# Mask matmuls, a new order of loads, and a regrouped first output phase in an attention and feed-forward kernel

## The chip, the cores and the metric

The kernel runs on one core of one Trainium2 chip. The metric is the device time of one execution in microseconds (us). Every execution also comes with the mean clock that was granted to TensorE, 1.0 being full speed. The five engines are TensorE (PE in the profile; PEld is its loading of weights), VectorE (DVE), ScalarE (ACT), GpSimd (POOL) and SyncE (SP). The program gives each of them a queue of instructions of its own. PSUM is the memory that the matmuls of this kernel write to; the kernel divides it into eight banks of 512 fp32 values in each of 128 partitions. SBUF is the memory that holds the other operands.

A ratio below is the mean time of one kernel's fast runs over the mean of the other kernel's fast runs of the same rounds, so it is not quite the ratio of the medians that stand beside it.

## The reference, cut to what matters

```python
# 8 batches, 8 heads, 512 local and 32 global positions, head size 64
k_all, v_all = concat(k_g, k_l), concat(v_g, v_l)
out_g = softmax(q_g @ k_all.T / 8) @ v_all            # global rows see everything
s_ll  = where(abs(i - j) <= 32, q_l @ k_l.T / 8, -1e9)  # local rows: a band of 65 ...
s_l   = concat(q_l @ k_g.T / 8, s_ll)                 # ... and the global columns
out_l = softmax(s_l) @ concat(v_g, v_l)
x = concat(out_g, out_l) as [8 * 544, 512]
h = x @ w_in                                          # 512 -> 2048, the "first layer" of a batch
out = (h * sigmoid(1.702 * h)) @ w_out                # 2048 -> 512, the "output phase" of a batch
```

## The kernel before

Four heads of a batch are a *quad*; quads 0 and 1 are batch 0, quads 2 and 3 batch 1. In the code `a` is the first quad of a batch and `c` the second. The steps of a quad, cut:

```python
psS = tile_pool("psS", bufs=1, PSUM)    # one tile of four banks: the score tile "s4"
psP = tile_pool("psP", bufs=4, PSUM)    # four single banks, taken in turn: pbank()

S(rnd)   # scores of half of the keys, 16 matmuls, into the score tile
X(rnd)   # exp of them, PSUM -> SBUF, on ScalarE (1.6 us)
M(rnd)   # times the band mask, on VectorE (0.9 us)
K, XK    # scores of the global keys, and their exp
ekU(u), U(u)  # attention times values: unit 0 is the denominator, 1 and 2 the values
R        # 1/denominator, spread: transpose, reciprocal, transpose, on VectorE (1.7 us)
XL(0), XL(1)  # xL = ov * rs, on VectorE; the input of the first layer
gg, eg, Gm, G # the same for the global rows: matmuls into og (Gm), division (G)
```

Some more names of the code: rq and rk are q and k as loaded, g the global rows, ov what U writes, sT and rs the first and last result of R, fc the number of a step of the first layer.

The global rows of batch 1 are loaded in fp32 by the SP queue and cast on ScalarE:

```python
def load_g32(b, names, hold=False, eng=None):
    ...
        t = g32[b, name] = consts.tile([128, 2, D], F32, ...)
        if hold:
            nc.vector.memset(t[:, :, 0:1], 0.0)   # the load waits for VectorE to get here
        (eng or nc.sync).dma_start(out=t, in_=s[:, 2 * b : 2 * b + 2, :])

def cast_g32(b, names):
    ...
            nc.scalar.activation(t[:, 2 * b : 2 * b + 2, :D], g32[b, name], AF.Copy)
```

The first layer and the output phase:

```python
def h_step(i, fc):                 # one of 16 steps of the first layer
    hp = pbank("hp")               # waits until the bank of four steps ago has been read
    h_mm(i, fc, hp, range(NKC))    # 4 matmuls of 512 columns
    ... ACT: th = tanh(hp);  DVE: gT[fc] = (th + 1) * hp

def o_mm(i, st):                   # one of 16 groups of 4 matmuls of 512 columns
    if first: ops[i, tci] = pbank("op")
    ...
```

The order of the start and of the first output phase, cut:

```python
c.S(0); c.X(0); a.M(1)
load_g32(1, "qkv", hold=True)            # at about 13 us
... c.S(1); c.X(1, halves=True) ... c.M(0) ... c.M(1, 0, 192); c.M(1, 192) ...
for fc in range(4, FC):                  # first layer of batch 0
    h_step(0, fc)
    if fc == 7:  cast_g32(1, "qkv")
    if fc == 10: transpose_g(2, 4)
...
osteps(0, (2, 2), (2, 3))                # first output phase, its second half
c.S(0); a.ekUs(c); c.XK(); c.X(0); a.U(0); a.R()
osteps(0, (3, 0))
a.U(1); a.U(2); c.S(1); a.Gm(); c.M(0); a.XL(0); a.XL(1); c.X(1); c.M(1); c.eg(); a.G()
osteps(0, (3, 1), (3, 2))
c.UG(); c.RXG()                          # the whole of the second quad's end
osteps(0, (3, 3))
```

The softmax here doesn't subtract the row's maximum and nothing guards it: scores larger than these inputs give would overflow.

## Time and profile before

The median was 313.07 us when the prediction was made (three runs, 312.66 to 313.36), and 312.94 with the run beside the changed kernel. The table gives the time at which each stage begins, read from the timeline as the start of its first matmul.

| stage | before, us |
|---|---|
| first scores | 7.90 |
| first layer, batch 0 | 20.19 |
| output phase, batch 0 | 34.41 |
| first layer, batch 1 | 57.08 |
| output phase, batch 1 | 73.19 |
| first layer, batch 2 | 93.10 |
| span of the profiled run | 310.7 |

The waits of TensorE (who waited, for whom, us in total, times, longest) are short:

```profile
PE w L162 <- DVE warm L158: 1.5, 1, 1.5
PE s L291 <- DVE kT L260: 0.9, 1, 0.9
PE kb L310 <- ACT e L319: 0.5, 1, 0.5
PE s L291 <- DVE q L263: 0.4, 1, 0.4
PE hp L457 <- DVE xL L421: 0.3, 1, 0.3
```

Four lines of the timeline of before (start, duration, engine, line, operation) show the way of the global rows of batch 1 and the seam between first layer and output phase. They are asked for at 12.95 us and cast at 28.19, without a wait; the output matmuls begin at 34.41, twenty of them in 4.48 us:

```profile
12.95 0.37 SPq L124 DMA_DIRECT2D g32q<-in_q_g_dram  x1
28.19 0.30 ACT L130 ACTIVATE rqg<-g32q 128x128 bf16<-128x128 f32 x1
28.59 0.30 ACT L130 ACTIVATE rvg<-g32v 128x128 bf16<-128x128 f32 x1
34.41 4.48 PE L482 MATMUL op<-w_out_sb,gT 128*128 128x512 bf16 x20
```

### The profile page before, as it was taken

What the parts mean: (1) busy time and instruction counts of PE and PEld (TensorE: products, weight loads), DVE (VectorE), ACT (ScalarE), POOL (GpSimd) and SP (SyncE); (2) the same over time, 40 slices, a digit from 0 to 9 for tenths busy, and PEclk for the clock granted to TensorE, in tenths of its full rate; (3) what the DMA queues carried; (4) which work ended last, traced back from release to release, by engine and by line L of the source; (5) the groups of instructions that cost most, each with busy time, mean ns of one, the idle gap of its engine ahead of it and who ended that gap; (6) DMA issues with size and microseconds to landing.
All of it is one profiled execution on the core that took longest, in us unless ns stands there. A gap on an engine that the chain in (4) does not pass through costs nothing.

```text
span 310.7 us, 7885 instructions
## 1 busy us (share of the span) xinstructions
PE 302.8 (97%) x3257; PEld 148.6 (48%) x3257; DVE 210.4 (68%) x463; ACT 167.3 (54%) x254; POOL 80.0 (26%) x131
## 2 busy tenths in 40 slices
PE   7899999999999999999999999999999999999995
PEld 6444444444554454444454455444454454446653
DVE  7887946869867866776957866776767855574320
ACT  4817465476536744565446735565556652563321
POOL 8822579677146000900045001200000000000000
PEclk9999999999999999999999999999999999999999
DMA  8999999999969212970279113901120012201123
GB/s 154 149 189 207 206 161 193 165 147 129 151 77 168 45 36 61 139 108 12 60 77 169 30 36 71 102 0 31 41 49 23 0 38 55 48 0 29 41 61 76
DMA packets 60099, 27.44 MB, mean 88 GB/s; under 512 B 43296, under 2 KB 51744, under 8 KB 60064
## 3 DMA queue, kind: packets, MB, share of 16 engines
q0 software_dynamic: 51536, 17.11, 50.7%
q1 hardware_dynamic: 7904, 9.12, 11.9%
q10 hardware_dynamic: 624, 0.72, 0.8%
q8 instruction: 25, 0.41, 0.5%
q14 instruction: 10, 0.08, 0.1%
HBM read 35.13 MB, written 8.91 MB: 142 GB/s over the span
## 4 chain that ended last, share of the span: by engine, by line
PE 91%; DVE 3%; ACT 2%; DMA 1%; POOL 1%; issue 0%; ACTq 0%; DVEq 0%; POOLq 0%
PE op L482 37%; PE hp L457 36%; PE s L291 6%; PE ov L389 5%; PE ov L367 3%; DMA rk<-in_k_l_dram 1%; PE s L457 1%; ACT e L322 1%; PE kb L310 1%; DVE e L329 1%; PE op L494 1%; PE s L310 1%; DVE gT L465 1%; PE s L406 1%; POOL rk L84 1%; PE ov L162 1%
## 5 line engine op out<-in xcount | busy, mean ns | idle before, releaser
L482 PE MATMUL op<-w_out_sb,gT 128*128 128x512 bf16 x528 | 121.9, 380 | 0.1
L465 DVE SCALAR_TENSOR_TENSOR gT<-th,hp 128x512 bf16<-128x512 f32 (+1 forms) x140 | 91.1, 655 | 43.0 <-ACT th L464 42.4
L457 PE MATMUL hp<-xL,w_in_sb 128*128 128x512 bf16 x496 | 108.6, 379 | 0.3 <-DVE xL L421 0.3
L464 ACT ACTIVATE th<-hp 128x512 f32<-128x512 f32 (+1 forms) x140 | 79.9, 573 | 43.7 <-PE hp L457 41.2
L457 PEld LDWEIGHTS <-w_in_sb 128*128 128x128 bf16 x576 | 56.1, 98 | 65.1 <-issue 1.2
L482 PEld LDWEIGHTS <-gT 128*128 128x128 bf16 x528 | 49.3, 98 | 56.2 <-issue 3.3
L322 ACT ACTIVATE e<-s 128x1712 bf16<-128x1712 f32 (+2 forms) x32 | 49.6, 1552 | 15.8 <-PE s L406 8.9
L496 ACT ACTIVATE ob<-op 128x512 f32<-128x512 f32 (+2 forms) x35 | 20.5, 585 | 61.6 <-PE op L482 59.1
L97 POOL DMA_DIRECT2D v<-in_v_l_dram x36 | 27.0, 757 | 96.2 <-PE s L406 88.9
L84 POOL DMA_DIRECT2D rk<-in_k_l_dram x64 | 34.9, 557 | 12.3 <-DMA w_in_sb<-in_moe_w_in_dram 4.7
L329 DVE TENSOR_TENSOR e<-e,mask 128x1408 bf16<-128x1408 bf16 (+2 forms) x33 | 28.0, 851 | 6.9 <-ACT e L322 6.7
L412 DVE STREAM_TRANSPOSE sT<-ov 128x512 f32<-128x512 f32 x16 | 11.4, 714 | 31.3 <-PE ov L389 31.3
L291 PE MATMUL s<-q,kT 32*128 32x200 bf16 (+1 forms) x512 | 21.3, 284 | 1.5 <-DVE kT L260 0.9
L421 DVE TENSOR_TENSOR xL<-ov,rs 128x512 bf16<-128x512 f32 x32 | 20.7, 685 | 2.2 <-PE ov L389 0.9
L291 PEld LDWEIGHTS <-kT 32*128 32x128 bf16 x512 | 10.9, 95 | 14.7 <-issue 9.1
L357 ACT ACTIVATE ek<-kb 128x512 bf16<-128x512 f32 x16 | 9.6, 600 | 8.4 <-PE kb L310 8.4
L389 PE MATMUL ov<-e,v 128*32 128x192 bf16 (+1 forms) x512 | 13.1, 240 | 0.0
L416 DVE STREAM_TRANSPOSE rs<-rT 128x512 f32<-128x512 f32 x16 | 11.4, 711 | 0.6
L260 DVE STREAM_TRANSPOSE kT<-rk 128x512 f32<-128x512 f32 (+1 forms) x17 | 11.4, 671 | 0.0
L263 DVE STREAM_TRANSPOSE q<-rq 128x512 f32<-128x512 f32 (+1 forms) x17 | 10.9, 647 | 0.0
L389 PEld LDWEIGHTS <-v 128*32 128x32 bf16 x512 | 9.8, 97 | 2.0 <-issue 2.0
L310 PE MATMUL kb<-q,kgT 32*32 32x512 bf16 x128 | 10.0, 385 | 0.5 <-ACT e L319 0.5
(71 smaller groups left out, 155.5 us busy)
## 6 DMA issues: line engine op xcount, KB each, us to landing
out_dram<-ob SPq DMA_DIRECT2D x132, 64.0 KB, 1.7
rk<-in_k_l_dram POOLq DMA_DIRECT2D x64, 64.0 KB, 4.0
v<-in_v_l_dram POOLq DMA_DIRECT2D x28, 128.0 KB, 4.5
rq<-in_q_l_dram POOLq DMA_DIRECT2D x6, 512.0 KB, 6.7
w_in_sb<-in_moe_w_in_dram POOLq DMA_DIRECT2D x4, 512.0 KB, 11.7
w_out_sb<-in_moe_w_out_dram POOLq DMA_DIRECT2D x4, 512.0 KB, 13.4
rq<-in_q_l_dram POOLq DMA_DIRECT2D x3, 256.0 KB, 7.9
q<-in_q_l_dram ACTq DMA_DIRECT2D x1, 512.0 KB, 3.9
```

The source lines that it names most:

```text
L84: nc.gpsimd.dma_start(out=loaded[b][0][32 * j : 32 * j + 32, u], in_=kf[b, j][:, u])
L97: nc.gpsimd.dma_start(out=vtiles[b % 2][p, s, :, :, :D], in_=vf[b, t][:, hs])
L291: nc.tensor.matmul(ps[j][:, off : off + n * nr], lhsT=self.k[p, 128 * c : 128 * c + 128, e], rhs=self.q[p, t0 : t0 + n, r0 : r0 + nr, e], ...
L322: nc.scalar.activation(e[:, :, lo:hi], self.ps[:, :, lo:hi], AF.Exp, scale=scale)
L329: nc.vector.tensor_mul(e, e, mask[:, rnd : rnd + 1, lo:hi].to_broadcast([128, 4, hi - lo]))
L389: nc.tensor.matmul(ov[32 * j : 32 * j + 32, :].rearrange("p (t r) -> p t r", t=16)[:, :, r0 : r0 + nr], lhsT=lv, rhs=self.E[c // 2][:, j, ...
L421: nc.vector.tensor_mul(self.x[:, 2 * self.u + h, :], self.st[1 + h], self.st["rs"])
L457: nc.tensor.matmul(hp[:, : width(i)], lhsT=w_in_c[:, fc // 8, kc, fc % 8 // 2, :, fc % 2], rhs=(xL[i] if i < B else xG)[:, kc, :], start=( ...
L464: nc.scalar.activation(th[:, :n], hp[:, :n], AF.Tanh, scale=0.851)
L465: nc.vector.scalar_tensor_tensor(gTs[i][:, fc, :n], in0=th[:, :n], scalar=1.0, in1=hp[:, :n], op0=ALU.add, op1=ALU.mult)
L482: nc.tensor.matmul(op, lhsT=gTs[i][:, fc, tci * 128 : tci * 128 + 128], rhs=w_out_sb[:, fc, :], start=(first and fc == 4 * f4), stop=(fc = ...
L496: nc.scalar.activation(ob[:, lo:hi], op[:, lo:hi], AF.Copy, scale=0.5)
```

## The change: its intent and the diff

The change means to take work out of the two places where TensorE was not full. It has three parts.

*Start.* The band masks of batch 0 are added to the scores on TensorE, as a large negative number, before exp, so that VectorE need not multiply. Half of the first keys come through SP in fp32, q in two pieces, v in eight, w_in in eight pieces, and the quarters of w_out come in a new order. The second scores of quad 1, with their mask matmuls, are cut in halves, as its exp already was.

*Global rows of batch 1.* They are loaded later, so that they do not get in the way of what the start needs; their casts and transposes move back with them.

*First output phase.* Scores of quad 3 come earlier, and its attention-times-values goes into the four banks of the score tile, so that the output matmuls can go on beside it. In the second layer quad 3's G is put after step 1, and some later pieces of work move back by one step (not in the cut below).

```diff
-    nc.scalar.dma_start(out=q32, in_=qf[0][:, 0])
+    for hf in range(2): ... nc.scalar.dma_start(out=q32[:, f], in_=qf[0][:, 0, f])
+    for j in range(4):
+        nc.sync.dma_start(out=k32[32 * j : 32 * j + 32], in_=kf[0, j][:, 0, 0:2])
 ...
-    keep(62, psP.tile([128, 512], F32, name="w", tag="p"), 128)
+    keep(40, psP.tile([128, 512], F32, name="w", tag="p"), 128)      # dummy matmuls
 ...
+        def B(self, rnd, split=False, cs=(0, 1)):      # masks: perm.T @ bias into the scores
+            ...
+                    nc.tensor.matmul(ps[j][:, w : w + 16 * WIN[c][1]], lhsT=perm, rhs=window(bias, c), ...)
 ...                                                    # start: the M of batch 0 go, B come
-    a.ekU(1, 3)
-    c.S(1)
-    c.X(1, halves=True)
+    c.B(1, cs=(0,)); c.S(1, added=True, cs=(0,)); c.X(1, part=0)
+    a.U(1); a.XL(0)
+    c.B(1, cs=(1,)); c.S(1, added=True, cs=(1,)); c.X(1, part=1)
 ...
-    load_g32(1, "qkv", hold=True)                      # was after c.X(0)
     for fc in range(4, FC):
         h_step(0, fc)
-        if fc == 7:
+        if fc == 5:
+            load_g32(1, "qkv", hold=True)
+            mps = pbank("mp") ...                      # mask of the later batches, once
+        if fc in (6, 7, 8, 9):
+            make_mask(fc - 6, mps)                     # on ScalarE
+        if fc == 11:
             cast_g32(1, "qkv")
-        if fc == 10:
+        if fc == 14:
             transpose_g(2, 4)
 ...                                                    # first output phase
+    c.S(0); c.X(0); c.M(0)
     osteps(0, (2, 2), (2, 3))
+    c.S(1); a.ekUs(c, 1); c.X(1); c.XK()
+    for unit in range(3): a.U(unit)
+    a.R(); c.M(1); c.eg()
+    pt = psS.tile([128, 4, 512], F32, name="s4")
+    a.Gm(pt[:, 0, 0 : D + 2])
+    osteps(0, (3, 0), (3, 1))
+    a.XL(0); a.XL(1)
+    c.ekUs(banks=[pt[:, unit + 1, :] for unit in range(3)])
+    for unit in range(3): c.U(unit)
+    c.R(); c.XL(0); c.XL(1)
+    a.G()
+    c.Gm(pt[:, 0, 256 : 256 + D + 2])
+    osteps(0, (3, 2), (3, 3))
```

More of the change, by code (lines that the diff above doesn't have):

```diff
@@ L135 @@
     q32 = ld.tile([128, 16 * D], F32, name="q32", bufs=1)
-    nc.scalar.dma_start(out=q32, in_=qf[0][:, 0])
-    load_g32(0, "qk")
-    load_g32(0, "v", eng=nc.scalar)
-    for j in range(4):
-        load_k(0, 0, j)
-    mk = consts.tile([32, 208], BF16)
-    nc.vector.memset(mk, 1.0)
-    for sg, base in ((1, 2 * W + 3), (-1, -3)):
-        nc.gpsimd.affine_select(
-            out=mk, in_=mk, pattern=[[-sg, 208]], compare_op=ALU.is_ge,
-            fill=0.0, base=base, channel_multiplier=4 * sg,
-        )
+    for hf in range(2):
+        f = slice(8 * D * hf, 8 * D * hf + 8 * D)
+        nc.scalar.dma_start(out=q32[:, f], in_=qf[0][:, 0, f])
+    k32 = ld.tile([128, 2, 4 * D], F32, name="k32", bufs=1)
+    load_g32(0, "q")
+    for j in range(4):
+        nc.sync.dma_start(out=k32[32 * j : 32 * j + 32], in_=kf[0, j][:, 0, 0:2])
+    load_g32(0, "kv")
+    step = consts.tile([128, 257], BF16)
+    nc.vector.memset(step, 1.0)
+    nc.gpsimd.affine_select(
+        out=step, in_=step, pattern=[[1, 257]], compare_op=ALU.is_ge,
+        fill=0.0, base=-65, channel_multiplier=-1,
+    )
+    for j in range(4):
+        nc.gpsimd.dma_start(out=loaded[0][0][32 * j : 32 * j + 32, 0, 2:4], in_=kf[0, j][:, 0, 2:4])
     load(0, (1,))
@@ L173, with rows4, window, make_mask @@
     WIN = ((0, 10), (6, 12), (14, 12), (22, 10))
-    mb = consts.tile([128, 16, 12], BF16)
     mask = consts.tile([128, 2, LW], BF16)
-    def make_mb():
-        for k in range(4):
-            nc.vector.tensor_copy(mb[32 * k : 32 * k + 32],
-                                  mk[:, 3 - k : 195 - k].rearrange("p (r t) -> p t r", t=16))
-    def make_mask():
-        at = 0
-        for c, (r0, nr) in enumerate(WIN):
-            lo = r0 - 8 * c + 2
-            nc.scalar.activation(
-                mask[:, c // 2, at : at + 16 * nr].rearrange("p (t r) -> p t r", t=16),
-                mb[:, :, lo : lo + nr], AF.Copy)
-            at = (at + 16 * nr) % LW
+    BIG = 262144.0
+    perm = consts.tile([128, 128], BF16)
+    band = consts.tile([128, 192], BF16)
+    bandt = consts.tile([128, 16, 12], BF16)
+    bias = consts.tile([128, 16, 12], BF16)
+    def rows4(t):
+        return t.rearrange("p (r t) -> p t r", t=4)
+    nc.vector.tensor_sub(perm.rearrange("p (t r) -> p t r", t=4), rows4(step[:, 65:193]), rows4(step[:, 64:192]))
+    nc.vector.tensor_sub(band, step[:, 65:257], step[:, 0:192])
+    nc.vector.tensor_scalar(bias, band.rearrange("p (r t) -> p t r", t=16), -1.0, BIG, op0=ALU.add, op1=ALU.mult)
+    def window(t, c):
+        lo = 0 if c else 2
+        return t[:, :, lo : lo + WIN[c][1]]
+    def make_mask(c, ps):
+        nr = WIN[c][1]
+        at = (0, 160, 0, 192)[c]
+        nc.scalar.activation(mask[:, c // 2, at : at + 16 * nr].rearrange("p (t r) -> p t r", t=16),
+                             window(ps[:, 0:192].rearrange("p (t r) -> p t r", t=16), c), AF.Copy)
     ones32 = consts.tile([128, 32], BF16)
@@ L214, in load_rest @@
     def load_rest():
-        load_v(0)
-        for part in range(2):
-            cs = slice(part * (d_ff // 2), (part + 1) * (d_ff // 2))
+        for u in range(2):
+            load_v(0, (u,))
+        for c4 in range(4):
             for u in range(2):
-                nc.gpsimd.dma_start(out=w_in_sb[:, part, 2 * u : 2 * u + 2, :], in_=w_in_r[u][:, :, cs])
-        for g4 in range(4):
+                lo = c4 % 2 * 512
+                nc.gpsimd.dma_start(out=w_in_sb[:, c4 // 2, 2 * u : 2 * u + 2, lo : lo + 512],
+                                    in_=w_in_r[u][:, :, 512 * c4 : 512 * c4 + 512])
+        for g4 in (1, 0, 2, 3):
             nc.gpsimd.dma_start(
@@ L223, in load_rest @@
                 in_=w_out_r[:, 2 * g4 : 2 * g4 + 2, :])
-            if g4 == 1:
+            if g4 == 0:
                 load(1, (0,))
@@ L249, in __init__ @@
             self.E = [None, None]
+            self.bk = {}
             self.st = {}
@@ L275, in ext, with S @@
                     qgT[:, self.Q, : n * nr].rearrange("p (t r) -> p t r", t=n))
-        def S(self, rnd, split=False, warm=0):
-            if split:
-                ps = [pbank("s") for _ in range(4)]
-                keep(warm, ps[0])
-            else:
-                pt = self.spt(rnd)
-                ps = [pt[:, j, :] for j in range(4)]
-            off = 0
-            for c in (2 * rnd, 2 * rnd + 1):
+        def B(self, rnd, split=False, cs=(0, 1)):
+            if cs[0] == 0:
+                self.bk[rnd] = [pbank("s") for _ in range(4)] if split else self.spt(rnd)
+            ps = self.bk[rnd] if split else [self.bk[rnd][:, j, :] for j in range(4)]
+            for c in [2 * rnd + i for i in cs]:
+                w = (40, 200, 36, 228)[c]
+                for j in range(4):
+                    nc.tensor.matmul(ps[j][:, w : w + 16 * WIN[c][1]], lhsT=perm, rhs=window(bias, c),
+                                     start=(c == 2 * rnd), stop=False, skip_group_check=True)
+        def S(self, rnd, split=False, added=False, cs=(0, 1)):
+            if not added and cs[0] == 0:
+                self.bk[rnd] = self.spt(rnd)
+            ps = self.bk[rnd] if split else [self.bk[rnd][:, j, :] for j in range(4)]
+            for c in [2 * rnd + i for i in cs]:
+                off = (0, 200, 0, 228)[c]
                 r0, nr = WIN[c]
@@ L294, in S @@
                             rhs=self.q[p, t0 : t0 + n, r0 : r0 + nr, e],
-                            start=(e == 0), stop=(e == 1), skip_group_check=True,
+                            start=(e == 0 and not added), stop=(e == 1), skip_group_check=True,
                         )
-                off += n * nr
+            if cs[0] == 0:
+                self.E[rnd] = att.tile([128, 4, RW + 32], BF16, name="e%d" % rnd)
             if split:
                 self.gk(ps[2][:, RW : RW + 32], self.qg)
-            self.ps = ps if split else pt
-            self.E[rnd] = att.tile([128, 4, RW + 32], BF16, name="e%d" % rnd)
+            self.ps = self.bk[rnd]
         def gk(self, out_, rhs, e=None):
@@ L312, in gk, with X @@
                                      start=(ee == 0), stop=(ee == 1), skip_group_check=True)
-        def X(self, rnd, halves=False):
+        def X(self, rnd, part=None):
             e = self.E[rnd]
@@ L320, in X @@
                 return
-            for lo, hi in ((0, 228), (228, RW)) if halves else ((0, RW),):
+            for lo, hi in ((0, RW),) if part is None else ((228 * part, 228 + 200 * part),):
                 nc.scalar.activation(e[:, :, lo:hi], self.ps[:, :, lo:hi], AF.Exp, scale=scale)
-            if rnd == self.gr:
+            if rnd == self.gr and not part:
                 nc.scalar.activation(e[:, 2, RW:], self.ps[:, 2, RW : RW + 32], AF.Exp, scale=scale)
@@ L349, in spt, with gg @@
             return self.pt
-        def gg(self):
-            self.gr = 0
-            self.gk(self.spt(0)[:, 2, RW : RW + 32], self.qg)
+        def gg(self, rnd=0):
+            self.gr = rnd
+            self.gk((self.ps if rnd else self.spt(0))[:, 2, RW : RW + 32], self.qg)
         def XK(self):
@@ L357, in XK, with ekU @@
             nc.scalar.activation(self.ek, self.kb, AF.Exp, scale=scale)
-        def ekU(self, unit, warm=0):
-            ov = self.st[unit] = pbank("ov")
+        def ekU(self, unit, warm=0, ov=None):
+            if ov is None:
+                ov = pbank("ov")
+            self.st[unit] = ov
             keep(warm, ov)
@@ L368, in ekU, with ekUs @@
                                  start=True, stop=False, skip_group_check=True)
-        def ekUs(self, nxt=None):
+        def ekUs(self, nxt=None, rnd=0, banks=(None, None, None)):
             if nxt:
-                nxt.gg()
+                nxt.gg(rnd)
                 nxt.K(0)
-            self.ekU(0)
+            self.ekU(0, ov=banks[0])
             if nxt:
                 nxt.K(1)
-            self.ekU(1)
-            self.ekU(2)
+            self.ekU(1, ov=banks[1])
+            self.ekU(2, ov=banks[2])
         def U(self, unit):
@@ L393, in U, with Gm @@
                     )
-        def Gm(self, nxt=None):
-            og = nxt.pt[:, 0, RW : RW + D + 2] if nxt else pbank("og")
+        def Gm(self, og=None):
+            if og is None:
+                og = pbank("og")
             for c in range(5):
@@ L439, in UG @@
                 self.U(unit)
-            self.Gm(nxt)
+            self.Gm(nxt and nxt.pt[:, 0, RW : RW + D + 2])
         def RXG(self):
@@ L517, in cast_q @@
         nc.scalar.activation(rq[:, 0, f], q32[:, f], AF.Copy)
-    make_mb()
     cast_q(0)
     cast_q(1)
-    make_mask()
+    nc.scalar.activation(rk[:, 0, 0:2], k32, AF.Copy)
     cast_g32(0, "q")
@@ L533 @@
     load_rest()
-    a.S(0)
+    a.B(0)
+    a.B(1, split=True)
+    a.S(0, added=True)
     a.X(0)
-    a.S(1, split=True, warm=4)
+    a.S(1, split=True, added=True)
     a.X(1)
     c.ext()
+    c.Tk()
     cast_g32(0, "v")
-    c.Tk()
+    c.Tq()
+    c.B(0)
     a.K()
     a.XK()
-    a.M(0)
-    c.Tq()
+    c.S(0, added=True)
     c.gg()
-    c.S(0)
     c.X(0)
-    a.M(1)
-    load_g32(1, "qkv", hold=True)
     a.eg()
-    c.K(0)
+    c.K()
+    c.XK()
     a.ekU(0)
-    c.K(1)
-    c.XK()
     a.U(0)
     a.R()
-    a.ekU(1, 3)
-    c.S(1)
-    c.X(1, halves=True)
-    a.ekU(2, 4)
-    a.U(1)
+    nc.vector.tensor_copy(bandt, band.rearrange("p (r t) -> p t r", t=16))
+    a.ekU(1, 2)
+    c.B(1, cs=(0,))
+    c.S(1, added=True, cs=(0,))
+    c.X(1, part=0)
+    a.U(1)
+    a.XL(0)
+    c.B(1, cs=(1,))
+    c.S(1, added=True, cs=(1,))
+    c.X(1, part=1)
+    a.ekU(2)
     a.U(2)
+    a.XL(1)
     a.Gm()
-    c.M(0)
-    a.XL(0)
-    c.M(1, 0, 192)
-    c.M(1, 192)
-    a.XL(1)
     gTs[0] = moe.tile([128, FC, TB], BF16, name="gT")
@@ L595 @@
         h_step(0, fc)
-        if fc == 7:
+        if fc == 5:
+            load_g32(1, "qkv", hold=True)
+            mps = pbank("mp")
+            nc.tensor.matmul(mps[:, 0:192], lhsT=perm, rhs=bandt.rearrange("p t r -> p (t r)"),
+                             start=True, stop=True)
+        if fc in (6, 7, 8, 9):
+            make_mask(fc - 6, mps)
+        if fc == 11:
             cast_g32(1, "qkv")
-        if fc == 10:
+        if fc == 14:
             transpose_g(2, 4)
@@ L615 @@
     osteps(0, (0, 1), (0, 0), (1, 1), (1, 0), (2, 1))
-    c.ext()
     a.S(0)
@@ L623 @@
     a.eg()
+    c.T()
+    c.ext()
     osteps(0, (2, 0), (0, 2), (0, 3))
@@ L626 @@
     a.X(1)
-    c.T()
     a.M(1)
     osteps(0, (1, 2), (1, 3))
+    c.S(0)
+    c.X(0)
+    c.M(0)
     osteps(0, (2, 2), (2, 3))
-    c.S(0)
-    a.ekUs(c)
+    c.S(1)
+    a.ekUs(c, 1)
+    c.X(1)
     c.XK()
-    c.X(0)
-    a.U(0)
+    for unit in range(3):
+        a.U(unit)
     a.R()
-    osteps(0, (3, 0))
-    a.U(1)
-    a.U(2)
-    c.S(1)
-    a.Gm()
-    c.M(0)
+    c.M(1)
+    c.eg()
+    pt = psS.tile([128, 4, 512], F32, name="s4")
+    a.Gm(pt[:, 0, 0 : D + 2])
+    osteps(0, (3, 0), (3, 1))
     a.XL(0)
     a.XL(1)
-    c.X(1)
-    c.M(1)
-    c.eg()
+    c.ekUs(banks=[pt[:, unit + 1, :] for unit in range(3)])
+    for unit in range(3):
+        c.U(unit)
+    c.R()
+    c.XL(0)
+    c.XL(1)
     a.G()
-    osteps(0, (3, 1), (3, 2))
-    c.UG()
-    c.RXG()
-    osteps(0, (3, 3))
+    c.Gm(pt[:, 0, 256 : 256 + D + 2])
+    osteps(0, (3, 2), (3, 3))
     a, c = nq[2]
@@ L658 @@
         h_step(1, fc)
+        if fc == 1:
+            nq[1][1].G()
         if fc == 2:
@@ L662 @@
             a.Tq()
-        if fc == 7:
+        if fc == 8:
             transpose_g(4, 6)
             a.ext()
-        if fc == 9:
+        if fc == 10:
             a.S(0)
@@ L671 @@
             a.X(0)
-        if fc == 12:
+        if fc == 13:
             a.M(0)
```

## The prediction

> **What bounds it now.** The page gives TensorE 302.8 of 310.7 us busy, and the chain of waits is TensorE for 91%. From 57 us on the chain is back-to-back matmuls: 64 of 512 columns take 13.81 us, 215.8 ns each[...]. No step there changes; only the first 57 us can give time.
>
> - Start: the timeline has the first scores at 7.90 us, after a DMA of rk (3.08 to 7.06 in the chain), and the first layer at 20.19. Between them useful TensorE work is about 7 us (four score rounds of 0.60, two K of 0.43, six ekU+U of 0.5, small ones): 5 us are waits and 11 dummy matmuls of 0.22. Mask multiplies of 0.89 us stand in the chain.
> - First output phase: 34.41 to 57.08, 22.7 us. The same work later (107.1 to 127.7) takes 20.6. So 2.1 us are lost here, around the unoverlapped second quad (e, sT, rs, xL, 51.3 to 57.1).
> - DMA: full in the page's slices to about 85 us, at 150 to 210 GB/s. By issue plus time to landing: v of batch 0 is in at 15.7, w_in in four parts at 18.8, 21.7, 24.6, 27.4 (the last just as fc 8 needs it), w_out at 30, 32.5, 37.7, 40.5, q of quad 3 at 42.9, where its transpose starts at once. Just in time throughout.
>
> **What the change does.** Removes four mask multiplies (0.85 to 0.95 us DVE each) and 1.33 us of mask copies; adds 16 matmuls per quad of 160 to 192 columns, 0.59 us per round (estimate: columns at 215.8 ns per 512). Quad 0's run while TensorE waits for data anyway; quad 1's largely while ACT runs exp (1.6 us). Mask building moves into the first layer (about 1.3 us ACT, which has 0.27 us slack per step).
>
> The first scores now wait for q and half of k: estimated 6.8 us (-1.1). [...] Then exp of 1.6, 1.8, 0.6, 1.8, 0.6, 1.65 us on ACT becomes the chain; I get the first layer at 17.5 (-2.7). w_in in eighths should arrive at 17.1, 18.6, 20, 21.4...: enough, with up to 0.5 us of wait at fc 4. The first layer ends near 31.6 instead of 34.4.
>
> The regrouped phase by itself would recover nearly all of its 2.1 us, but loads move only 0.5 to 1 us earlier: w_out's last quarter near 40 and q of quad 3 near 42.4 now stop TensorE, about 1 us each. I expect 21.5 to 22.7 us for the phase and the second layer at 53.7 (-3.4) at best, -2 if DMA holds it. Behind that everything shifts.
>
> **Prediction: 310.0 us**, 80% range 307.9 to 311.9. Faster by over 2% 0.04, within 2% 0.95, slower 0.01.
>
> **What would show it.** First scores at 6.4 to 7.2 us; first layer at 17 to 18; its waits small, on w_in if any; waits in the output phase on w_out or q/k transposes; later phases unchanged (20.6, 13.8 us); ACT's lag in the first layer about 1 us more without stopping TensorE.
>
> **What would make it wrong.** Loads come clearly earlier because late g loads and smaller pieces free the engines: then up to -5 us. Or w_in in eighths costs bandwidth or POOL issue time: the first layer starves and the gain falls to 1 us or less. Mask matmuls on the chain (1.2 us) would cost a third of the start's gain.

The two passages that are cut hold no term of the sum. It stands as it was on record: the first layer 2.7 us earlier, the second layer 3.4 at best and 2 if the loads hold it, all behind it shifted; from 313.07 us that is 309.7 to 311.1, and 310.0 was put on record.

## More of the kernel before

The page of the kernel before, its parts 1 and 2. In part 2 each digit is one of 40 slices of the span, in tenths:

```profile
span 310.7 us, 7885 instructions
PE 302.8 (97%) x3257; PEld 148.6 (48%) x3257; DVE 210.4 (68%) x463; ACT 167.3 (54%) x254; POOL 80.0 (26%) x131
...
PEclk9999999999999999999999999999999999999999
DMA  8999999999969212970279113901120012201123
```

TensorE is the bound, the DMA engines are full for the first quarter, and the clock stays at 9 tenths or more in every slice.

## The result, and the profile after

The changed kernel took 327.74 us (median of four runs, 325.68 to 329.89) against 312.94 (four runs); the ratio is 1.0472, with a 95% interval of 1.0399 to 1.0546. I had predicted a small gain; it is a loss of 15 us.

| stage begins, us | before | after | stage before it became longer by |
|---|---|---|---|
| first scores | 7.90 | 7.55 | |
| first layer, batch 0 | 20.19 | 21.69 | 1.5 (start) |
| output phase, batch 0 | 34.41 | 42.41 | 6.5 (first layer, 6.2 of it a wait at its end) |
| first layer, batch 1 | 57.08 | 71.70 | 6.6 (output phase) |
| output phase, batch 1 | 73.19 | 89.19 | 1.4 |
| first layer, batch 2 | 93.10 | 109.10 | 0.0 |
| span | 310.7 | 326.5 | -0.2 after that |

So everything was lost before 89 us, in the places that were to gain. The page after shows a clock that falls three times in the first 75 us:

```profile
span 326.5 us, 7905 instructions
PE 307.9 (94%) x3259; PEld 150.0 (46%) x3259; DVE 207.0 (63%) x458; ACT 168.2 (52%) x255; POOL 84.3 (26%) x138
...
PEclk9799969969999999999999999999999999999999
DMA  8999999999712951198028901580121011200213
```

Two waits of TensorE are new and long (the page's first group of output matmuls shows the same 6.2 us):

```profile
PE op L509 <- DVE gT L492: 6.2, 1, 6.2
PE s L433 <- DVE xg L455: 3.6, 1, 3.6
PE s L301 <- ACT e L346: 1.6, 2, 1.0
```

**The first wait.** The waits of ScalarE between 30 and 45 us, and the timeline around them, tell where it comes from:

```profile
ACT rkg L130 <- DMA g32k<-in_k_g_dram: 2.5, 1, 2.5
ACT rqg L130 <- DMA g32q<-in_q_g_dram: 2.5, 1, 2.5
ACT rvg L130 <- DMA g32v<-in_v_g_dram: 1.7, 1, 1.7
```

```profile
28.88 0.38 SPq L124 DMA_DIRECT2D g32q<-in_q_g_dram  x1
35.93 0.31 ACT L130 ACTIVATE rqg<-g32q 128x128 bf16<-128x128 f32 x1 [2.54 <-DMA g32q<-in_q_g_dram]
38.78 0.31 ACT L130 ACTIVATE rkg<-g32k 128x128 bf16<-128x128 f32 x1 [2.54 <-DMA g32k<-in_k_g_dram]
40.84 0.31 ACT L130 ACTIVATE rvg<-g32v 128x128 bf16<-128x128 f32 x1 [1.75 <-DMA g32v<-in_v_g_dram]
41.06 0.58 ACT L491 ACTIVATE th<-hp 128x512 f32<-128x512 f32 x1
42.41 6.47 PE L509 MATMUL op<-w_out_sb,gT 128*128 128x512 bf16 x20 [6.20 <-DVE gT L492]
```

The rows are now asked for at 28.88 to 31.25 us and land 7.0 to 9.6 us later. Their casts stand in ScalarE's queue after step 11 and wait for them. The tanh of step 12 stands behind the casts and runs at 41.06 instead of near 33.7, when step 11's was done. The tanh of steps 12 to 15, with the product on VectorE (gT) behind it, is what gives back the four PSUM banks that the steps hold, and the first output matmul needs one of them. So TensorE stands from 36.2 to 42.4. The order is the program's in this trace: the casts at 35.93, 38.78 and 40.84, and tanh at 41.06, directly behind the last of them.

**The second wait.** The timeline before the second layer shows the second Gm (L433, into the score tile) wait for VectorE:

```profile
64.40 0.72 DVE L439 STREAM_TRANSPOSE sT<-s 128x512 f32<-128x512 f32 x1 [1.04 <-PE s L415]
66.19 1.29 DVE L448 TENSOR_TENSOR xL<-s,rs 128x512 bf16<-128x512 f32 x2
67.58 0.28 DVE L455 TENSOR_SCALAR xg<-s,rg 128x64 bf16<-128x64 f32 x1
67.92 0.41 PE L433 MATMUL s<-v,e 128*32 128x66 bf16 x16 [3.57 <-DVE xg L455]
68.32 3.59 PE L509 MATMUL op<-w_out_sb,gT 128*128 128x512 bf16 x8
```

**The clock.** After both waits the matmuls are slow: 20 output matmuls take 6.47 us (4.48 before), 8 take 3.59 (the eight at 53.31 us in the same phase took 1.90). The view by stretches (busy us of each engine with its number of instructions, then the granted clock, the DMA share and GB/s) shows the clock at one half:

```profile
35.00:40.00 5.00, 1.21 (x6) 0.46 (x5) 0.00 (x0) 0.62 (x2) 2.29 (x5) 0.97 1.15 205
40.00:45.00 5.00, 2.59 (x7) 0.92 (x7) 3.10 (x5) 3.19 (x6) 3.07 (x5) 0.50 1.44 166
65.00:70.00 5.00, 2.08 (x25) 0.88 (x25) 2.97 (x8) 0.00 (x0) 2.61 (x4) 0.70 0.88 126
66.60:67.00 0.40, 0.00 (x0) 0.00 (x0) 0.40 (x2) 0.00 (x0) 0.00 (x0) 0.95 0.71 90
67.00:67.40 0.40, 0.00 (x0) 0.00 (x0) 0.40 (x2) 0.00 (x0) 0.00 (x0) 0.50 1.04 78
```

At the first wait the granted clock was 1.00 from 39.0 to 39.4 us, 0.81 from 39.4 to 39.8 and 0.50 from 39.8 to 46.4; TensorE had been without a matmul since 36.2. At the second it fell sooner, after 2.6 us without a matmul (the last two lines above; see the last section). The prediction has no term for the clock.

**Theories.** Theory 1: the two waits and the half clock after each make nearly all of the loss, and each wait has one cause that can be taken away by itself (the place of the casts in a queue; a tile that two writers share). Its rivals: the loads as a whole are late, so that w_out, q or k would hold TensorE in any case; TensorE needs the late rows themselves; the wait before Gm is only the wait for xL that would come a little later; the low clock has another cause than idleness.

### The profile page after: what moved, and what is told of

The parts are those of the page before. It is cut to its first block, busy times and chain, and to the rows that moved or that the text cites. A ratio compares the mean times of both kernels' runs of the same rounds, so it can differ in the third digit from the quotient of the medians.

```text
span 326.5 us, 7905 instructions
## 1 busy us (share of the span) xinstructions
PE 307.9 (94%) x3259; PEld 150.0 (46%) x3259; DVE 207.0 (63%) x458; ACT 168.2 (52%) x255; POOL 84.3 (26%) x138
## 4 chain that ended last, share of the span: by engine, by line
PE 84%; DMA 6%; DVE 3%; POOL 3%; ACT 2%; issue 1%; ACTq 0%; SPq 0%; DVEq 0%
PE op L509 36%; PE hp L484 30%; PE s L315 6%; PE ov L415 5%; DMA g32v<-in_v_g_dram 3%; PE ov L393 3%; DMA rq<-in_q_l_dram 2%; DVE gT L492 1%; DMA rk<-in_k_l_dram 1%; PE s L484 1%; POOL rk L84 1%; POOL v L97 1%; PE kb L334 1%; ACT e L346 1%; ACT th L491 1%; PE s L433 1%
## 5 line engine op out<-in xcount | busy, mean ns | idle before, releaser
L509 PE MATMUL op<-w_out_sb,gT 128*128 128x512 bf16 x528 | 125.6, 388 | 6.3 <-DVE gT L492 6.2
L484 PE MATMUL hp<-xL,w_in_sb 128*128 128x512 bf16 x496 | 109.8, 381 | 0.0
L509 PEld LDWEIGHTS <-gT 128*128 128x128 bf16 x528 | 50.1, 99 | 65.3 <-issue 14.1
L97 POOL DMA_DIRECT2D v<-in_v_l_dram x40 | 28.9, 731 | 112.6 <-PE s L433 105.0
L84 POOL DMA_DIRECT2D rk<-in_k_l_dram x60 | 32.5, 548 | 8.9 <-DMA w_in_sb<-in_moe_w_in_dram 4.4
L353 DVE TENSOR_TENSOR e<-e,mask 128x1408 bf16<-128x1408 bf16 x28 | 24.4, 872 | 8.3 <-ACT e L346 8.3
L448 DVE TENSOR_TENSOR xL<-ov,rs 128x512 bf16<-128x512 f32 x30 | 19.4, 686 | 3.7 <-PE ov L415 2.1
L415 PE MATMUL ov<-e,v 128*32 128x160 bf16 (+1 forms) x480 | 12.3, 239 | 0.0
```

The lines of the kernel that those rows point to most:

```text
L84: nc.gpsimd.dma_start(out=loaded[b][0][32 * j : 32 * j + 32, u], in_=kf[b, j][:, u])
L97: nc.gpsimd.dma_start(out=vtiles[b % 2][p, s, :, :, :D], in_=vf[b, t][:, hs])
L353: nc.vector.tensor_mul(e, e, mask[:, rnd : rnd + 1, lo:hi].to_broadcast([128, 4, hi - lo]))
L415: nc.tensor.matmul(ov[32 * j : 32 * j + 32, :].rearrange("p (t r) -> p t r", t=16)[:, :, r0 : r0 + nr], lhsT=lv, rhs=self.E[c // 2][:, j, ...
L448: nc.vector.tensor_mul(self.x[:, 2 * self.u + h, :], self.st[1 + h], self.st["rs"])
L484: nc.tensor.matmul(hp[:, : width(i)], lhsT=w_in_c[:, fc // 8, kc, fc % 8 // 2, :, fc % 2], rhs=(xL[i] if i < B else xG)[:, kc, :], start=( ...
```

## The experiments

There were seventeen kernels, all correct (a planned e3 was not run). Times are medians; "before" in each job was 312.7 to 313.3 us.

**e1: the early load put back.** From the changed kernel:

```diff
     c.X(0)
+    load_g32(1, "qkv", hold=True)
     a.eg()
 ...
         if fc == 5:
-            load_g32(1, "qkv", hold=True)
```

> The changed kernel, with one thing undone: the global rows of batch 1 are loaded after exp of quad 1 (as before the change), not from step 5 of the first layer. Theory 1 (ScalarE stands in its queue at the casts of those rows, 35.3 to 40.8 us, so tanh of steps 12 to 15 comes late, the PSUM banks stay taken and TensorE stands 6.2 us): that wait goes, and with it the half clock after it; 319.0 to 320.5 us. Rival (the loads as a whole are late; w_out or q and k would hold TensorE anyway): the wait only moves to another load, 325 us or more.

Measured: 319.65 us (ratio 1.021). The wait before the output phase is gone, and the first 20 output matmuls are at full clock again (the trace has a record of 19 of them):

```profile
35.94 4.48 PE L509 MATMUL op<-w_out_sb,gT 128*128 128x512 bf16 x19
```

8.1 us of the 14.8 are explained. No wait for w_out, q or k came in its place, so the first rival falls.

**e2: G ahead of R.** From the changed kernel:

```diff
         c.U(unit)
+    a.G()
     c.R()
     c.XL(0)
     c.XL(1)
-    a.G()
     c.Gm(pt[:, 0, 256 : 256 + D + 2])
```

> The changed kernel, with the division of quad 2's global rows (G) put on VectorE ahead of quad 3's R and XL, so that the second Gm, which writes the same PSUM bank, need not wait for the end of VectorE's queue. Theory 1: TensorE's wait of 3.6 us before the second Gm goes, and most of the half clock after it (about 2 us); 322 to 323.5 us. Rival (TensorE would wait for xL of quad 3 a little later anyway, since R and XL end at 67.5 us): at most 1.5 us, 326 us.

Measured: 329.30 us, no gain; my expectation was wrong. The wait did not go away, it changed its partner. The timeline of e2 has the second Gm here:

```profile
69.25 0.41 PE L433 MATMUL s<-v,e 128*32 128x66 bf16 x16 [3.83 <-DVE xL L448]
```

XL reads banks 2 and 3 of the score tile. Gm writes to bank 0. That does not look like a wait for a bank.

**e4: dummies in the first gap.**

```diff
+    keep(28, pts[0][:, 0, :])      # 28 matmuls of 512 columns into bank 0 of the score tile
     osteps(0, (0, 1), (0, 0), (1, 1), (1, 0), (2, 1))
```

> The changed kernel with 28 dummy matmuls of 512 columns (6 us at full clock) put on TensorE between the first layer and the first output phase, where it stands idle 6.2 us. If the half clock after the gap is a cost of its own, made by the idleness: the first 20 output matmuls take 4.3 us instead of 6.5, and the time falls by 2 to 3 us to 325. If the lower clock has another cause, or costs nothing that the chain sees: no change, 327.7, or longer if the dummies don't fit.

Measured: 335.15 us. The test of the clock failed, because the dummies did not run in the gap but after it:

```profile
42.99 8.20 PE L166 MATMUL s<-warm 128*128 128x512 bf16 x27 [7.67 <-DVE gT L535]
```

They were written to bank 0, whose last reader was long done; they waited for L535, which at that point reads banks 2 and 3 of the same tile. Together with e2 this gives the second theory its form: a write to a tile waits for every read of the tile that was issued before it, whichever banks it touches. If that is so, it is an order that the program's dependency tracking makes, not one that the data need; e16 tests it directly.

**e5: the late load alone, in the kernel before.**

```diff
-    load_g32(1, "qkv", hold=True)
 ...
-        if fc == 7:
+        if fc == 5:
+            load_g32(1, "qkv", hold=True)
+        if fc == 11:
             cast_g32(1, "qkv")
-        if fc == 10:
+        if fc == 14:
             transpose_g(2, 4)
```

> The kernel before, with this one part of the change: the global rows of batch 1 are loaded from step 5 of the first layer, cast after step 11 and transposed after step 14. Theory 1 (lateness of this load is enough by itself): TensorE stands 5 to 7 us before the output phase, and 319 to 323 us result. Rival (it takes the smaller pieces and the mask work on ScalarE as well): under 315 us.

Measured: 320.85 us (ratio 1.025), with TensorE's wait of 6.5 us before the output phase. This move of a load of 192 KB, with its casts and transposes, costs 8 us by itself, the half clock included:

```profile
41.10 7.34 PE L482 MATMUL op<-w_out_sb,gT 128*128 128x512 bf16 x19 [6.51 <-DVE gT L465]
```

The mask work on ScalarE and the smaller pieces are not needed for it.

**e6: e1 with Gm issued early.**

```diff
         c.U(unit)
+    c.Gm(pt[:, 0, 256 : 256 + D + 2])
     c.R()
 ...
     a.G()
-    c.Gm(pt[:, 0, 256 : 256 + D + 2])
```

> e1 (early global rows) with quad 3's Gm issued before its R and XL, not after. Theory 1 (a write to one bank of the four-bank score tile waits for every read of that tile that was issued before it, whichever bank it reads: in e2 the wait went over from G to XL, in e4 the dummies in bank 0 waited for a read of banks 2 and 3): now nothing has read the tile's ov banks before Gm, so the 3.6 us go and most of the half clock after it, less up to 0.9 us of wait for xL at the second layer: 314 to 315.5 us against e1's 319.65. Rival (TensorE waits for xL there in any case): 318 us or more.

Measured: 314.38 us (ratio 1.0041). The wait is gone and 5.3 us with it. With e1 that is 13.4 of the 14.8 us. The regrouped output phase now takes 21.78 us (36.60 to 58.38) against 22.67 before.

**e7: e1 with TensorE kept busy in the second gap.**

```diff
+    keep(16, pbank("fill"))
     c.Gm(pt[:, 0, 256 : 256 + D + 2])
```

> e1 with 16 dummy matmuls of 512 columns (3.5 us at full clock) on TensorE just before quad 3's Gm, into a free bank of the other pool, so that TensorE is busy in the wait and nothing else changes. If the half clock after the gap comes from the idleness: the 8 output matmuls after it take 1.8 us instead of 3.6 and the time is about 317.3 us. If it doesn't: 319.6 us.

Measured: 316.83 us, 2.8 us less than e1 with 16 matmuls more. The wait is as long as before, only filled. The eight output matmuls after it take 1.90 us:

```profile
55.29 3.63 PE L166 MATMUL fill<-warm 128*128 128x512 bf16 x16
59.21 1.90 PE L509 MATMUL op<-w_out_sb,gT 128*128 128x512 bf16 x8
```

So the low clock is a cost of its own, made by the idleness: of the 5.3 us that e6 wins, about half is the wait and about half is the clock after it.

**e8 and e9: the regrouped output phase alone, in the kernel before.** e8 takes that part of the change as it is; e9 issues Gm early as in e6.

> The kernel before with the regrouped output phase alone (loads, start and masks as before). Theory 1: it brings the wait of 3.6 us and the half clock after it into the kernel before, less about 1 us that the regrouping gains: 316 to 318.5 us. Rival (the regrouping loses only because the loads of the changed kernel are late): 311 to 313 us.

> e8 with quad 3's Gm issued before R and XL. Theory 1: without the wait the regrouping is worth what I had predicted or a little less: 311.5 to 312.7 us against 312.7 before. If it is over 313 the regrouping itself costs time.

Measured: e8 318.86 us (ratio 1.0178), a little above the range that I expected, with the same wait of 3.6 us; e9 313.94 us (ratio 1.0019, interval 0.9982 to 1.0056), which is in the range that I had set for "the regrouping itself costs time", although the interval holds 1. The regrouping without its wait gains 0.9 us in the output phase (21.78 instead of 22.67). The second layer gives it back: 17.35 us instead of 16.11, for waits of 0.6 us for xL and 0.5 us for copies into q.

**e10: e9 without those waits.**

```diff
-    c.ekUs(banks=[pt[:, unit + 1, :] for unit in range(3)])
+    c.ekUs(banks=[None, pt[:, 2, :], pt[:, 3, :]])     # denominator in a bank of the other pool
 ...
-        if fc == 8:
+        if fc == 7:
             transpose_g(4, 6)
```

> e9 with two more steps: the denominators of quad 3 go to a bank of the other pool (so that R waits for them alone, not for every write to the score tile), and the transposes of the global rows come one step earlier in the second layer. In e9 the second layer began 0.9 us earlier after its start than before, but took 1.2 us more: 0.57 us of waits for xL, 0.5 us for the copies into q. If these waits are where the gain of the regrouping went: 312.0 to 312.8 us, 0.5 us or more under before. If not: 313.5 or more.

Measured: 313.50 us (ratio 0.9986, interval 0.9947 to 1.0025): the median is the one that I had set for "if not", but the interval holds 1, so the times leave it open; the stages do not. The second layer is back to 16.07 us and the phase stays at 21.79. R's first step now starts 0.06 us after the last denominator matmul (56.38 us, a wait of 0.43 for it); in e9 it started 0.85 us after it (54.92), behind Gm's matmuls. The six runs fall in two groups: two at 311.5 us with a mean clock of 0.999 or more, four at 313.4 to 314.0 with 0.992 to 0.995. The kernel before did the same in that job: eight runs at 312.4 to 313.0 us and full clock, three at 314.3 to 314.8 with about 0.995. The profiled run of e10 is one of the slower ones, and its clock falls in the start:

```profile
12.00:14.00 2.00, 0.97 (x28) 0.47 (x27) 1.65 (x6) 0.72 (x2) 1.52 (x3) 1.00 2.26 157
14.00:16.00 2.00, 1.67 (x30) 0.65 (x19) 0.99 (x3) 1.91 (x3) 1.66 (x3) 0.58 1.14 124
```

**e11, e12, e13: the new start alone.** e11 is e1 with the output phase of before. e12 also loads v, w_in and w_out as before. e13 is e11 with B, S and X of quad 1's second round undivided:

```diff
-    c.B(1, cs=(0,)); c.S(1, added=True, cs=(0,)); c.X(1, part=0)
-    a.U(1); a.XL(0)
-    c.B(1, cs=(1,)); c.S(1, added=True, cs=(1,)); c.X(1, part=1)
+    c.B(1); c.S(1, added=True); c.X(1)
+    a.U(1); a.XL(0)
```

> The changed kernel with early global rows and the output phase of before: what is left is the new start (masks on TensorE, new order and size of the loads). If the start loses by itself, as the first layers at 21.0 to 22.8 us in five runs against 20.2 to 21.2 with the old start say: 314 to 315.5 us. If it is neutral and e6 was slow because of the regrouping: 313 us or less.

> e11 with v, w_in and w_out loaded in the sizes and order of before (w_in in four pieces, not eight; v in four, not eight). If the pieces hold the start back (the first piece of w_in is issued at 12.2 us instead of 10.4, and the timeline of e1 shows TensorE wait 1.0 us for the third piece): first layer 0.5 to 1 us earlier, 313 to 314 us. If the score chain does: no change against e11.

> e11 with mask matmuls, scores and exp of quad 1's second round undivided. In the changed kernel the second half's mask matmuls wait for the exp of the first half (a write to the score tile behind a read of it, other banks' columns or not), 0.6 and 1.0 us of TensorE's wait. If that wait holds the start: exp ends 0.5 to 0.8 us earlier and the time falls by as much against e11. If the first layer then waits for w_in instead: no change.

Measured: e11 313.91 us (ratio 1.0025, interval 0.9985 to 1.0065), e12 313.41 (1.0022), e13 313.68 (1.0011). All three intervals hold 1, so of each alone it can only be said that it does not gain what I had predicted. At full clock (0.997 or more) the means are 314.0 us for e11 (four runs), 313.2 for e12 (three), 312.9 for e13 (two), against 312.6 for the eight of before; that is a hint that both undone parts help a little, not more. The traces show what is in the way. In e11 and e13 TensorE waits 0.7 and 1.1 us for w_in; in e12 it does not. In the changed kernel the second half's mask matmuls wait for the first half's exp, the tile rule of e2 and e4 again (0.6 us; the wait of 1.0 us that I had also counted here is quad 1's first mask matmul behind quad 0's exp, and stays in e13):

```profile
16.86 0.93 ACT L346 ACTIVATE e<-s 128x912 bf16<-128x912 f32 x1 [1.56 <-PE s L315]
17.85 0.44 PE L301 MATMUL s<-bias,perm 128*128 128x160 bf16 x4 [0.62 <-ACT e L346]
```

**e14: dummies in the start of e10.**

```diff
+    keep(3, pbank("fill"))
     c.gg()
     c.S(0)
```

> e10 with three dummy matmuls of 512 columns before quad 1's first scores, where TensorE waits 0.4 to 1.6 us for q. In e10 two runs at a mean clock of 0.999 or more took 311.5 us and four at 0.992 to 0.995 took 313.4 to 314.0; the kernel before shows the same split (312.4 to 313.0 at full clock, 314.3 to 314.8 below). If idleness of TensorE in the start makes the split: nearly all runs at full clock, 311.3 to 312.0. If not: the split stays, median 313 or so.

Measured: 312.12 us (six runs, 311.86 to 312.34, all at 0.997 or more; ratio 0.9963, interval 0.9934 to 0.9992). The slower group is gone, as it should be if idleness makes it, at the price of about 0.6 us in each run (e10's two fast ones took 311.5). The median is just above what I expected. In e14's trace TensorE is busy throughout the four us of which it was idle for 1.4 in e10's, and the clock stays up:

```profile
12.00:14.00 2.00, 2.00 (x54) 0.97 (x54) 1.15 (x6) 1.54 (x2) 1.89 (x3) 1.00 2.16 160
14.00:16.00 2.00, 2.00 (x26) 0.83 (x25) 1.93 (x4) 1.51 (x4) 1.42 (x3) 1.00 1.20 150
```

The kernel before had its slower runs in this job too (three of eleven). Dummies alone in the kernel before were not run, so how much of e14's gain they make by themselves is open.

**e15: the whole change, mended** (e1, Gm early and the denominator's bank, B, S and X undivided, loads of v and w as before, the transposes of the second layer one step earlier).

> The changed kernel with all that was found mended: early global rows, Gm early and R's bank of its own, exp of the second round undivided, v and w loaded as before. If the masks on TensorE are worth something once the rest is out of the way: 311 us or less (below e10's full-clock 311.5). If the start as changed loses what the masks gain: 311.5 to 312.5 at full clock.

Measured: 311.88 us (ratio 0.9982, interval 0.9939 to 1.0025). Four runs at 0.997 or more took 311.4 to 312.3 us, two at 0.989 took 314.0 and 314.2. Its first layer began at 19.93 us, the earliest but one of all profiles. The four runs at full clock have a mean of 311.6 us, against 311.5 for e10's two: the new start, masks included, shows no gain over the old one. What the masks alone are worth was not measured.

**e16: the bank changed, the order not.** From e1:

```diff
-    c.Gm(pt[:, 0, 256 : 256 + D + 2])
+    c.Gm()                             # a bank of the other pool
```

> e1 with quad 3's Gm left where the change has it, after R, XL and G, but written to a bank of the other pool. If the 3.6 us in e1 are a wait of a write to the score tile for reads of other parts of the same tile: they go without any move, 314 to 315 us as e6. If the place in the order is what matters: 319 us or more.

Measured: 313.80 us (312.85 to 315.13), as e6. Gm stands where the change has it, behind R, XL and G, and runs without waiting, before XL (56.54 us in that timeline):

```profile
54.53 0.30 PE L433 MATMUL og<-v,e 128*32 128x66 bf16 x16
54.79 1.90 PE L509 MATMUL op<-w_out_sb,gT 128*128 128x512 bf16 x8
56.54 1.29 DVE L448 TENSOR_TENSOR xL<-s,rs 128x512 bf16<-128x512 f32 x2
```

That shows that it was the shared tile. XL reads banks 2 and 3, which Gm does not write. G reads bank 0 itself, in other columns than Gm writes; whether that read alone would have held Gm up was not shown.

**e17: late rows, but the casts behind the layer.** From the changed kernel:

```diff
-        if fc == 11:
-            cast_g32(1, "qkv")
-        if fc == 14:
-            transpose_g(2, 4)
 ...
     a.T()
+    cast_g32(1, "qkv")
+    transpose_g(2, 4)
     a.ext()
```

> The changed kernel with the global rows of batch 1 loaded as late as in the change, but their casts (and transposes) put behind the whole first layer on ScalarE's and VectorE's queues. If what cost 6.2 us is that tanh of steps 12 to 15 stood behind the casts on ScalarE: tanh now runs on, the 20 output matmuls start at once at full clock, and only the scores wait for the rows, some 2 us: 320 to 323 us. If TensorE needs the rows themselves at that time: 327 us or more.

Measured: 318.95 us, 8.8 us less than the changed kernel, although the rows come as late as there (7.1 to 10.6 us from request to landing). The profiled run is the slowest of the four (321.82): in its start the clock was 0.61 from 12 to 14 us and 0.50 from 14 to 16. All tanh runs before the casts, and the output matmuls start at once and at full clock:

```profile
37.62 4.48 PE L509 MATMUL op<-w_out_sb,gT 128*128 128x512 bf16 x20
38.69 0.60 ACT L491 ACTIVATE th<-hp 128x512 f32<-128x512 f32 x1 [0.97 <-DVE gT L492]
39.18 0.30 ACT L130 ACTIVATE rqg<-g32q 128x128 bf16<-128x128 f32 x1
40.43 0.31 ACT L130 ACTIVATE rkg<-g32k 128x128 bf16<-128x128 f32 x1 [0.95 <-DMA g32k<-in_k_g_dram]
42.03 0.66 PE L315 MATMUL s<-q,kT 32*128 32x200 bf16 x16
```

Even the scores of quad 2 follow the output matmuls without a wait. So TensorE never needed the rows at that time. What cost 6.2 us was the order in ScalarE's queue.

**e18: e15 with four dummies in its start**, before quad 1's first scores.

> e15 with four dummy matmuls of 512 columns before quad 1's first scores, where TensorE waits 0.9 us for q. e15 ran at 311.4 to 312.3 us in four runs at full clock and at 314.0 and 314.2 in two at 0.989. If idleness in the start makes the lower clock, as e14 says: all runs at 0.997 or more, median 311.3 to 311.9, under the kernel before by 0.3 to 0.5 per cent. If the split stays: a median near 312 with single runs at 314.

Measured: 312.12 us (311.47 to 312.40, all at 0.997 or more; ratio 0.9956, interval 0.9933 to 0.9979). It is a little above what I expected. It and e14 are the two versions that beat both kernels with an interval that lies below 1, by about 0.4%. In e18's job, though, four of the eleven runs of the kernel before took 313.6 to 314.1 us at 0.999 or more, for a reason that is not known, so idleness in the start does not explain every slow run, and part of e18's 0.4% may be theirs. e14 and e18 do not differ from each other, although e14 has none of the new start: what seems to be left of the change's gain is the regrouped output phase, with the dummies, which the change did not have, to keep the start warm.

## Why the prediction was wrong

*What bounds the kernel, and that all behind the second layer stays as it was.* Right. From the second output phase to the end both profiles have the same lengths (19.9 us to the third layer).

*"ACT's lag in the first layer about 1 us more without stopping TensorE."* This is the step that failed worst: TensorE was stopped for 6.2 us. I counted ScalarE's added work (mask building, 1.3 us) and found it small, which it is: e1 keeps it and has no wait. I did not ask what the moved casts wait for. The profile before had the answer. The same rows, asked for at 12.95 to 14.81 us, took 9.1 to 13.2 us to land there, which could be read in the view of the DMA issues. Step 5 of the first layer, by my own timetable, is at about 22 us, so they could not land before 31, and the cast after step 11 would come at about 27. I even named the late loads as a possible gain ("because late g loads ... free the engines"). In the runs the wait is 6.2 us, and with the half clock after it about 8 (e1: 8.1; e5: 8 alone; e17: 8.8).

*"The regrouped phase by itself would recover nearly all of its 2.1 us."* Wrong twice. First, I read the diff by the data: Gm and the readers of the other banks touch different columns, so I saw no wait. In these runs the order between instructions is kept by tile (e2, e4 and e16: waits of 3.8, 7.7 us and none), and the second Gm was issued behind R, XL and G: 3.6 us of wait, and 5.3 us with the clock that follows (e6; e8 shows 5.8 on the kernel before). Second, with that wait gone the phase gains 0.9 us and not 2, and at first the second layer gave all of it back (e9); with two more steps it is kept (e10, e14).

*"The first layer at 17.5 (-2.7)."* Wrong, and not because of one thing. It began at 21.69 us, 1.5 us later than before. The first scores came 0.35 us earlier instead of 1.1: the last piece of the first keys landed at 6.3 us, and a cast and a transpose follow. Quad 1's q landed at 11.3 us instead of 10.6 (5.2 us after its request, against 3.9), so its scores began at 12.1 instead of 11.8; with half of the first keys on the SP queue the loads moved 153 GB/s over the first 16 us, against 150 before, and I had no term for a later q. Exp of the second round lost its overlap to the tile rule (a wait of 0.6 us of TensorE). And in the profiled run the clock fell (0.59 from 12 to 14 us, 0.56 from 14 to 16, against 1.00 before), with fewer dummy matmuls and more waits than before. In e11 to e13 and e15 the new start as a whole shows no gain over the old one. How the loss divides between these, and what the masks bring, is not settled: the intervals are wider than the terms.

*"w_out's last quarter near 40 and q of quad 3 near 42.4 now stop TensorE, about 1 us each."* Wrong; no run shows those waits; TensorE came there later than I thought (the output phase began at 34.3 us or later in every run, not at 31.6), which is the likely reason. *"w_in ... up to 0.5 us of wait at fc 4"* was roughly right: none in the changed kernel, 0.7 to 1.1 us in e1, e11 and e13.

*The clock.* It is missing from the prediction altogether. The profile before shows full clock throughout, and I took it for given. In the changed kernel it costs about 2 us after the first wait (6.47 against 4.48 us for 20 matmuls) and 2.8 after the second (e7).

The sum: 8.1 us for the queue order (e1), 5.3 for the shared tile (e6, both with their clock), together 13.4 of 14.8; the 1.4 us that are left are the start, less what the regrouping gains.

## What to carry to other kernels

When an instruction that waits for a load is moved in an engine's queue, work out when the load will land from its measured time to landing, and ask what stands behind the instruction. Here 0.9 us of casts held up tanh, tanh held the PSUM banks, and TensorE stood 6 us. When work of two strands is put into one tile, ask in which unit the order is kept: a bank of its own (e16) cost nothing and took away 3.6 us of wait. And add to a gap on TensorE what the half clock costs after it: here 2.0 us after the gap of 6.2 us, and 2.8 us after the gap of 3.6 us. If the gap cannot be closed, dummy matmuls in it can be worth having (e7: 2.8 us less than e1; e14: all six runs at a clock of 0.997 or more, against two of six in e10).

## What these traces show of the clock, the loads and the order in PSUM

- The granted clock fell after 2.6 us without matmuls (64.4 to 67.0 us in the changed kernel, where it was 0.95 from 66.6 to 67.0 us and 0.50 from 67.0) and after 2.5 us in e1 (55.9 to 58.4; 0.71 from 58 to 59 us). In the starts of e10 and of the changed kernel it fell (to 0.58 and 0.59) with no single wait over 1.6 us, TensorE being busy for 1.9 us of the 4 before the fall in e10 (10 to 14 us) and for 2.2 of 4 in the changed kernel (8 to 12 us). In the kernel before TensorE was busy for 3.1 us of 8 to 12, and the clock stayed at 1.00. At which share of busy time it falls these runs do not show: e1 had 2.4 of 4 us (8 to 12) and stayed at 1.00.
- From the first matmul after the gap until the clock was full again it took 4.1 us at the first gap (42.4 to 46.5) and 5.9 us at the second (67.9 to 73.8).
- A sustained stream of matmuls of 512 columns with their weight loads took 215.8 ns for each at full clock (64 in 13.81 us, in both kernels).
- SP's 64 KB loads of the global rows of batch 1 took 7.0 and 9.4 us to land in the changed kernel and 9.1 and 11.6 in the kernel before, while GpSimd's loads were under way (DMA share 1.17 and 203 GB/s from 28.9 to 38.8 us in the changed kernel, 1.23 and 161 from 13 to 19 in the kernel before). In e1, asked for at 12.08 and 12.56 us, they took 2.8 and 5.4.
- Order in PSUM was kept by tile, not by bank: e2, e4 and e16 show it, with waits of 3.8, 7.7 us and none.
